# Linear attention into a squared-relu MLP: batch 2's first matmul in seven products, and one written-out order of all operations

## The chip, the cores and the metric

The kernel runs on one core of one Trainium2 chip. The metric is device time in microseconds (us) of one execution. Five engines matter: TensorE (PE in the profile, with PEld for its weight loads), VectorE (DVE), ScalarE (ACT), GpSimd (POOL) and SyncE (SP), which issues most DMAs. Each runs its own instructions strictly in the order in which the program gives them, so the order is part of the kernel.

## What is computed

Per batch (8) and head (8), with sequence 576 and head size 64, and then one MLP over all 4608 rows:

```python
q_p = concat(relu(q) * cos_w, relu(q) * sin_w)      # 576 x 128, k_p alike
kv  = k_p.T @ v                                     # 128 x 64
z   = sum(k_p)                                      # 128
x   = (q_p @ kv) / (q_p @ z + 1e-6)                 # 576 x 64 per head, 8 heads side by side: 512
h   = x @ w_in                                      # 512 -> 2048
out = (relu(h) ** 2) @ w_out                        # 2048 -> 512
```

## The kernel before

**Tiles and stages.** A batch's 576 rows are four tiles of 128 rows and a tail of 64. The four tiles of batch m make MLP step m (512 columns of x); the tails of all eight batches make a ninth step, m = 8. For a batch the kernel loads q, k and v, makes the cosine and sine features (line 339 on ScalarE, line 343 on VectorE), casts v, forms kv (line 385), transposes the query features, multiplies (line 505, the function `att_num`; for tails two batches in one call, with tiles named qpt and qptT), divides (lines 517 to 520) and transposes x. From batch 2 on the transposes are DMAs on the SP queue (line 469 for queries, line 537 for x). Loads of inputs and stores of outputs share that queue.

**First matmul.** Steps 0 to 2 use 16 units: 4 matmuls of 512 columns (line 594), a relu on ScalarE (line 603), and a square on VectorE after every four units (line 611). From step `FIRST_7` on, which is 3 (line 1405), the first matmul is done in seven products of half-size blocks instead of eight (Strassen's way, in Winograd's form): `plan_gemm1_7` runs four groups u of seven products, each 4 matmuls of 256 columns (line 671). It needs sums of weight blocks, made once (line 629), and of input blocks (line 653, four per step). In each group ScalarE copies the fifth product aside (line 1095), copies one bank into another as a seed twice (line 1078) and makes two relus (line 687); VectorE adds the fifth product to two banks (line 694), takes the maximum with zero (line 711) and squares (line 611). Two groups share four banks in two lanes.

**Second matmul.** Steps 0 and 1 are plain (lines 747 and 761). From step 2 on it is in seven products as well: 14 halves of 8 matmuls of 256 columns (line 860), sums of g blocks on VectorE (line 839), and copies and adds to the output tile (lines 1160, 1170, 1183 on ScalarE, 1166 on VectorE). The last step's version, in `plan_gemm2` for m = 8, uses more banks and stores in pieces: half stores by line 794 and quarter stores by line 802, on POOL, SP and ScalarE's queue. There the products come in the order 1, 2, 6, 5, 7, 3, 4; the result of product 7 in bank Z is added to the output (line 1166) and copied twice into other banks as seeds for product 4 (line 1221).

**Order.** Every operation is an `add` call on a planner: engine or engines, a duration, what it reads and writes, a due time. `order` lets all engines work in a model: when an engine falls free it takes the ready operation that is due first. `SHIFTS` corrects the due times of single operations, by number. An operation that may run on VectorE or ScalarE (features and casts) is taken by the engine that is free first. The result is the order in which the instructions are put out. Input transfers have landing times written in by hand (`plan.given`, `plan_pool`).

```python
i = min((i for i in waiting[e] if ready[i] <= s + 0.02), key=lambda i: (due[i], i))
```

## Time and profile before

| | |
|---|---|
| median of 3 runs | 275.87 us (275.8 to 275.89) |
| the profiled execution | 275.83 us |
| its span, first to last instruction | 274.1 us |
| mean granted TensorE clock | 0.997 |
| busy: PE, DVE, ACT, POOL | 97%, 80%, 67%, 6% of the span |
| DMA | 53.37 MB, mean 195 GB/s |

The span is the time from the first to the last instruction of the profiled execution; its device time has what lies around it as well. Busy shares are of the span. In rows of groups the two numbers before the second bar are the busy time of the group in us and the mean of one in ns; behind it stands how long the engine was idle just before, and what ended that. In timelines the first two numbers are start and length in us.

### The profile page before, as it was taken

What the parts mean: (1) busy time and instruction counts of PE and PEld (TensorE: products, weight loads), DVE (VectorE), ACT (ScalarE), POOL (GpSimd) and SP (SyncE); (2) the same over time, 40 slices, a digit from 0 to 9 for tenths busy, and PEclk for the clock granted to TensorE, in tenths of its full rate; (3) what the DMA queues carried; (4) which work ended last, traced back from release to release, by engine and by line L of the source; (5) the groups of instructions that cost most, each with busy time, mean ns of one, the idle gap of its engine ahead of it and who ended that gap; (6) DMA issues with size and microseconds to landing.
All of it is one profiled execution on the core that took longest, in us unless ns stands there. A gap on an engine that the chain in (4) does not pass through costs nothing.

```text
span 274.1 us, 6518 instructions
## 1 busy us (share of the span) xinstructions
PE 266.7 (97%) x2626; PEld 207.3 (76%) x2626; DVE 219.6 (80%) x440; ACT 182.8 (67%) x330; POOL 15.3 (6%) x29
## 2 busy tenths in 40 slices
PE   8999999999999998999999999999999999999993
PEld 3687555565445477898899898998988888888882
DVE  0974877877967999999989999998999679889401
ACT  2976741796677778779978998995645665583122
POOL 1572100000000000000000000000000000000013
PEclk9999999999999999999999999999999999999998
DMA  7999999699899999999999999845113100300134
GB/s 212 331 206 285 320 252 360 192 270 291 233 286 289 177 227 256 278 306 204 294 360 181 225 339 263 142 117 169 38 41 136 39 0 2 153 2 0 80 115 115
DMA packets 87005, 53.37 MB, mean 195 GB/s; under 512 B 56928, under 2 KB 83936, under 8 KB 86976
## 3 DMA queue, kind: packets, MB, share of 16 engines
q1 hardware_dynamic: 80448, 44.38, 62.5%
q0 software_dynamic: 5392, 8.26, 13.5%
q8 instruction: 20, 0.33, 0.5%
q10 hardware_dynamic: 1136, 0.33, 0.5%
q14 instruction: 9, 0.07, 0.1%
HBM read 36.70 MB, written 9.44 MB: 168 GB/s over the span
## 4 chain that ended last, share of the span: by engine, by line
PE 89%; DMA 5%; DVE 2%; SPq 2%; issue 0%; ACT 0%; POOL 0%; POOLq 0%; DVEq 0%
PE bank L860 29%; PE bank L671 26%; PE bank L594 12%; PE bank L747 5%; PE bank L761 5%; PE abank L385 3%; PE abank L505 3%; DMA q<-in_q_dram 3%; PE bank L721 3%; DMA qptT<-qpt 3%; SPq L237 1%; PE bank L578 1%; PE bank L478 1%; DVE x L443 0%; PE bank L542 0%
## 5 line engine op out<-in xcount | busy, mean ns | idle before, releaser
L860 PEld LDWEIGHTS <-gT 128*128 128x128 bf16 x448 | 43.2, 98 | 5.5 <-issue 0.5
L611 DVE TENSOR_TENSOR gT<-gT 128x2048 bf16<-128x2048 bf16 (+1 forms) x34 | 40.2, 1188 | 5.8 <-ACT gT L603 5.6
L860 PE MATMUL bank<-w2sb,gT 128*128 128x256 bf16 x336 | 42.1, 273 | 0.0
L671 PE MATMUL bank<-xT,w1sb 128*128 128x256 bf16 x288 | 41.9, 273 | 0.0
L687 ACT ACTIVATE gT<-bank 128x512 bf16<-128x512 f32 x48 | 28.5, 599 | 18.7 <-PE bank L671 15.7
L671 PEld LDWEIGHTS <-w1sb 128*128 128x128 bf16 x384 | 36.6, 98 | 4.3
L694 DVE TENSOR_TENSOR gT<-bank,qpTp 128x512 bf16<-128x512 f32 x48 | 31.0, 684 | 7.7 <-PE bank L671 7.2
L860 PEld LDWEIGHTS <-gs 128*128 128x128 bf16 x336 | 32.7, 98 | 3.8
L594 PE MATMUL bank<-xT,w1sb 128*128 128x512 bf16 x148 | 35.1, 379 | 0.0
L603 ACT ACTIVATE gT<-bank 128x512 bf16<-128x512 f32 x40 | 23.4, 601 | 13.2 <-PE bank L594 13.2
L1078 ACT COPY bank<-bank 128x512 f32<-128x512 f32 x48 | 27.6, 582 | 6.0 <-PE bank L671 5.4
L671 PEld LDWEIGHTS <-w1t 128*128 128x128 bf16 x288 | 28.0, 98 | 3.3
L860 PE MATMUL bank<-w2t,gs 128*128 128x256 bf16 x224 | 28.2, 273 | 0.0
L671 PE MATMUL bank<-qpTp,w1t 128*128 128x256 bf16 x192 | 27.7, 273 | 0.0
L594 PEld LDWEIGHTS <-w1sb 128*128 128x128 bf16 x148 | 13.6, 98 | 13.5
L520 DVE TENSOR_TENSOR x<-abank,rden 128x512 bf16<-128x512 f32 x30 | 20.7, 691 | 1.0
L1095 ACT COPY qpTp<-bank 128x512 f32<-128x512 f32 x24 | 13.8, 593 | 8.1 <-PE bank L671 6.6
L1166 DVE TENSOR_TENSOR ysb<-bank,y 128x512 f32<-128x512 f32 x14 | 9.6, 687 | 9.5 <-PE bank L860 9.0
L794 POOL DMA_DIRECT2D out_dram<-ysb x4 | 2.4, 613 | 238.2 <-ACT ysb L1170 234.9
L339 ACT ACTIVATE kp<-k,cos_col 128x512 bf16<-128x512 f32 x19 | 13.2, 717 | 2.9 <-DMA k<-in_k_dram 2.9
L747 PE MATMUL bank<-w2sb,gT 128*128 128x512 bf16 x64 | 14.8, 379 | 0.0
L339 ACT ACTIVATE qp<-q,cos_col 128x512 bf16<-128x512 f32 x21 | 14.7, 715 | 0.1
(119 smaller groups left out, 418.9 us busy)
## 6 DMA issues: line engine op xcount, KB each, us to landing
out_dram<-ysb SPq DMA_DIRECT2D x16, 512.0 KB, 3.2
q<-in_q_dram SPq DMA_DIRECT2D x14, 512.0 KB, 7.1
v<-in_v_dram SPq DMA_DIRECT2D x14, 512.0 KB, 5.5
k<-in_k_dram SPq DMA_DIRECT2D x12, 512.0 KB, 7.4
w1sb<-in_moe_w_in_dram POOLq DMA_DIRECT2D x4, 512.0 KB, 9.3
w2sb<-in_moe_w_out_dram POOLq DMA_DIRECT2D x4, 512.0 KB, 16.5
k<-in_k_dram SPq DMA_DIRECT2D x1, 1024.0 KB, 6.0
q<-in_q_dram POOLq DMA_DIRECT2D x1, 1024.0 KB, 12.0
```

The costliest lines, as they stand in the source:

```text
L339: eng.activation(out=dst[ps, :, lo : lo + D], in_=src[ps], func=ACTF.Relu, scale=col[ps])
L520: nc.vector.tensor_tensor(out=x[:, :], in0=n4[:, :, :, 0:D].rearrange("p b (k l) d -> p b k l d", l=2), in1=rden[:, :] .rearrange("p b (k ...
L594: nc.tensor.matmul(out=out_, lhsT=w1sb[:, kb, hb * P : (hb + 1) * P], rhs=x_block(m, kb), start=(kb == 0), stop=(kb == KB - 1),)
L603: nc.scalar.activation(out=gT_of(m)[:, hb, :], in_=bank[to][:, :], func=ACTF.Relu)
L611: nc.vector.tensor_tensor(out=g, in0=g, in1=g, op=ALU.mult)
L671: nc.tensor.matmul(out=bank[to][:, s * W : (s + 1) * W], lhsT=lhs[:, kb, (2 * u + s) * P : (2 * u + s + 1) * P], rhs=rhs[:, kb, :], start= ...
L687: nc.scalar.activation(out=g_pair(m, i, j, u), in_=bank[to][:, :].rearrange("p (s c) -> p s c", s=2), func=ACTF.Relu,)
L694: nc.vector.tensor_tensor(out=g_pair(m, i, j, u), in0=bank[to][:, :].rearrange("p (s c) -> p s c", s=2), in1=in_five(u).rearrange("p (s c) ...
L747: nc.tensor.matmul(out=bank[FIRST_Y[tt]][:, :], lhsT=gT_of(0)[:, hb, tt * P : (tt + 1) * P], rhs=w2sb[:, hb, :], start=(hb == 0), stop=(hb ...
L860: nc.tensor.matmul(out=bank[to][:, s * DM2 : (s + 1) * DM2], lhsT=lhs[:, hb, s * P : (s + 1) * P], rhs=rhs[:, hb, :], start=(fresh and hb ...
L1078: add("ACT", psum, lambda: nc.scalar.copy(out=bank[b][:, :], in_=bank[a][:, :]), r=[("bank", a)], w=[("bank", b)])
L1095: add("ACT", psum, lambda u=u, Y=Y: nc.scalar.copy(out=in_five(u), in_=bank[Y][:, :]), r=[("bank", Y)], w=five)
```

## The change

Four things change. `FIRST_7` becomes 2, so that the first matmul of step 2 is in seven products too; the weight sums stand in the plan one step earlier, and the planner has 1,302 operations where it had 1,270. Squares of whole groups may run on ScalarE (`add_square`, `squared`). In the last step the two copies of line 1221 stand ahead of the add that reads the same bank, and an operation that reads a bank now depends on those that read it before. And `order`, with its due times and `SHIFTS`, goes: `ORDER` lists all operations by number, in the order in which they are put out, each with its engine (p PE, a ScalarE, v VectorE, g POOL, s SP). Some written-in landing times are smaller; with the order fixed they reach no instruction.

The diff, cut: of the list the lines that the prediction speaks of, and its end.

```diff
-SHIFTS = {
-    62: -4, 63: -2.8, 82: -5.8, 99: -12, 100: -12.4, 101: -15.2, 102: -10, 103: -8.2, 104: -3,
...
-}
+ORDER = """
+0p 11a 17v 20v 14a 15v 18v 16a 12v 13v 22a 21v 1p 31g 27a 26v 23p 38v 19a 28p 37v 36v 2p 3p 29a 39p
+40p 43v 44a 41p 24v 45p 42a 46p 25v 47p 30v 4p 32g 57p 48a 66v 5p 49p 65a 51p 58v 6p 71a 67p 50v 7p
...
+156p 314v 92g 133a 154p 139p 134a 157v 141p 155v 93g 181v 158p 315v 174a 142a 159p 178a 317v 160p
...
+264s 288a 206v 294v 209p 286v 173p 210a 291v 287v 292a 217p 215v 226p 293a 270v 214a 223p 289v 227a
...
+319p 452a 425s 368p 342v 448a 320p 310s 251v 255a 432v 321p 431a 430v 433a 454v 322p 447v 455s 449a
...
+573s 401a 464v 417a 334p 419a 607v 465s 335p 402v 403v 336p 575s 584a 501p 470s 420v 337a 517p 338v
+588a 474p 385v 610a 476p 421v 591a 611s 583v 586a 477p 387v 592a 497v 475p 478a 498v 344v 518p 606s
+479a 502p 500v 519a 596v 482p 589v 503a 595v 594a 483p 593v 328s 585v 520a 499v 471p 504a 725s 521p
...
+599p 527v 600p 724s 510p 601a 531v 509p 512v 484a 529p 612p 511v 554p 530a 613v 480p 555a 532a 538p
+347v 513p 422v 614p 553p 515v 481p 615v 514a 556a 537p 539a 346v 616s 557p 745v 540a 617p 558p 743v
...
+1245a 1166v 1260v 1259p 1174p 1177a 1268p 1262a 1227v 1178a 1269p 1261v 1264v 1179p 1270a 1266v
+1180p 1263v 1181p 1183v 1182p 1265v 1276p 1267v 1277p 1229v 1184v 1271p 1185s 1278a 1272p 1186p
+1187p 1282p 1188a 1273a 1283p 1189s 1274g 1279p 1275g 1284a 1285a 1280p 1294p 1281a 1289p 1286v
+1295a 1288g 1290p 1287g 1298p 1297g 1291v 1296g 1293s 1299a 1301a 1292s 1300s
+"""
@@ -75,6 +106,9 @@
 
         n = len(self.ops)
         deps = set()
+        for key in r:
+            if key[0] in ("bank", "T"):
+                deps.update(self.readers.get(key, ()))
         for key in r:
             if key in self.last_write:
                 deps.add(self.last_write[key])
@@ -95,62 +129,14 @@
         self.ops.append([eng, dur, fn, deps, due, lag, at, name])
...
-    def behind(self, i, a):
-
-        return 0.0 if self.ops[i][0] == self.ops[a][0] == ("PE",) else self.ops[i][5]
-
...
-    def order(self, t0):
...
     def run(self, t0):
-        for i in self.order(t0):
-            self.ops[i][2](self.by[i])
+        names = {"p": "PE", "a": "ACT", "v": "DVE", "g": "POOL", "s": "SP"}
+        order = [(int(x[:-1]), names[x[-1]]) for x in ORDER.split()]
+        place = {i: n for n, (i, _) in enumerate(order)}
+        assert len(place) == len(order) == len(self.ops)
+        for i, e in order:
+            assert e in self.ops[i][0] and all(place[d] < place[i] for d in self.ops[i][3])
+            self.ops[i][2](e)
 
 
 @with_exitstack
@@ -602,13 +588,19 @@
     def unit_relu(m, hb, to):
         nc.scalar.activation(out=gT_of(m)[:, hb, :], in_=bank[to][:, :], func=ACTF.Relu)
 
-    def square(m, u, plain, a=0, n=4):
-
+    def squared(eng, g):
+
+        if eng is nc.scalar:
+            eng.activation(out=g, in_=g, func=ACTF.Square)
+        else:
+            eng.tensor_tensor(out=g, in0=g, in1=g, op=ALU.mult)
+
+    def square(m, u, plain, a=0, n=4, eng=nc.vector):
         if plain:
             g = gT_of(m)[:, 4 * u + a : 4 * u + a + n, :]
         else:
             g = gT_of(m).rearrange("p (j h) c -> p j h c", j=2)[:, :, 2 * u : 2 * u + 2, :]
-        nc.vector.tensor_tensor(out=g, in0=g, in1=g, op=ALU.mult)
+        squared(eng, g)
 
 
 
@@ -921,6 +913,9 @@
         engs = EITHER if only is None else (only,)
         add(engs, tuple(cost(e, n, kind) for e in engs), lambda e: fn(ENG[e]), r=r, w=w)
 
+    def add_square(n, fn, w):
+        add(EITHER, (0.06 + n * 0.00053, 0.1 + n * 0.00083), lambda e: fn(ENG[e]), w=w)
+
     def plan_k(b, j, cos=None, sin=None):
         ps, gs = parts_of(b, j)
         out = lambda x: [("kp", j, x)] if j < J else [("kpt", g, x) for g in gs]
@@ -1027,7 +1022,7 @@
             k = 2 if plain and u == 3 else 4
             if n % k == k - 1:
                 a = n % 4 + 1 - k
-                add("DVE", 0.06 + 512 * k * 0.00053, lambda u=u, a=a, k=k: square(m, u, plain, a, k),
+                add_square(512 * k, lambda e, u=u, a=a, k=k: square(m, u, plain, a, k, e),
                     w=[key for x in order[n + 1 - k : n + 1] for i in range(2) for key in g_keys(m, i, x // HB2, (x % HB2,))])
             if n % 4 == 3:
                 if not plain and u % 2:
@@ -1112,7 +1107,7 @@
             if not apart:
                 add("DVE", 0.34, lambda u=u: in_max(m, u), w=g(1, 0) + g(1, 1))
             if not apart:
-                add("DVE", 1.14, lambda u=u: square(m, u, False), w=[key for i in range(2) for j in range(2) for key in g(i, j)])
+                add_square(2048, lambda e, u=u: square(m, u, False, eng=e), w=[key for i in range(2) for j in range(2) for key in g(i, j)])
             if u % 2:
                 plan_g_sums(m, 2 * u - 2, 2 * u + 2)
 
@@ -1213,13 +1208,13 @@
         prod(5, V)
         five(V)
         prod(7, Z)
-        last(Z, 1, 1, True)
-        store_half(1, 1, ("POOL", "POOL"))
 
         for sub in range(2):
             add("ACT", cost("ACT", 256, "psum"),
                 lambda sub=sub: nc.scalar.copy(out=half_bank(2 + sub)[:, sub, :], in_=half_bank(Z)[:, sub, :]),
                 r=[("bank", Z)], w=[("bank", 2 + sub)])
+        last(Z, 1, 1, True)
+        store_half(1, 1, ("POOL", "POOL"))
         prod(3, Y)
         last(Y, 0, 1, True)
         store_half(0, 1, ("SP", "SP"))
@@ -1265,7 +1260,7 @@
     T0, TM = 1.2, 15.4
 
     for key, at in (
-        (("k", 0), 6.8), (("k", 1), 6.8), (("kt", 0), 7.1), (("q01",), 8.9), (("vt", 0), 9.5),
+        (("k", 0), 6.8), (("k", 1), 6.8), (("kt", 0), 7.1), (("q01",), 8.9), (("vt", 0), 9.3),
         (("v", 0), 10.2), (("v", 1), 11.5), (("q23",), 13.0),
     ):
         plan.given[key] = at
@@ -1309,7 +1304,7 @@
         plan_q(0, j, src=[("q01",)])
         plan_qT_pe(0, j, j, 10.0 + 0.3 * j, "DVE" if j == 0 else "ACT")
     add("POOL", 0.1, gate, r=[("vt", 0)], due=0.0)
-    for i, at in enumerate((16.2, 19.4, 21.9, 24.5)):
+    for i, at in enumerate((15.6, 19.1, 21.1, 23.7)):
         plan_pool(at, lambda i=i: load_w1(i, 4), [("w1", i)])
     for half in range(2):
         for i in range(2):
@@ -1348,14 +1343,14 @@
         plan_num(0, j, TM + 0.5 + 0.8 * (j - 2))
         plan_x_pe(0, j, 2 + j, TM + 1.8 + 0.8 * (j - 2), None)
 
-    plan_pool(27.1, lambda: load_main("q", 1, nc.gpsimd), [("q", 0), ("q", 1), ("q01",), ("q23",)])
-    plan_pool(29.9, lambda: load_w2(0, 4), [("w2", 0)])
-    plan_pool(32.9, lambda: load_main("k", 1, nc.gpsimd), [("k", 0), ("k", 1)])
-    plan_pool(33.3, lambda: load_tail("k", 1, nc.gpsimd), [("kt", 1)])
-    plan_pool(35.6, lambda: load_w2(1, 4), [("w2", 1)])
-    plan_pool(38.6, lambda: load_main("v", 1, nc.gpsimd), [("v", 0), ("v", 1)])
-    plan_pool(39.0, lambda: load_tail("v", 1, nc.gpsimd), [("vt", 1)])
-    for i, at in ((2, 41.3), (3, 43.9)):
+    plan_pool(27.0, lambda: load_main("q", 1, nc.gpsimd), [("q", 0), ("q", 1), ("q01",), ("q23",)])
+    plan_pool(29.5, lambda: load_w2(0, 4), [("w2", 0)])
+    plan_pool(32.3, lambda: load_main("k", 1, nc.gpsimd), [("k", 0), ("k", 1)])
+    plan_pool(32.7, lambda: load_tail("k", 1, nc.gpsimd), [("kt", 1)])
+    plan_pool(35.1, lambda: load_w2(1, 4), [("w2", 1)])
+    plan_pool(38.1, lambda: load_main("v", 1, nc.gpsimd), [("v", 0), ("v", 1)])
+    plan_pool(38.6, lambda: load_tail("v", 1, nc.gpsimd), [("vt", 1)])
+    for i, at in ((2, 41.0), (3, 43.7)):
         plan_pool(at, lambda i=i: load_w2(i, 4), [("w2", i)])
     for s in FIRST_S:
         plan_first(s)
@@ -1363,7 +1358,7 @@
         n = hb - 4 * len(FIRST_S) // 2
         plan_unit(0, hb, n % 4, TM + len(FIRST_S) * dt0 + n * dt0 / 2)
         if n % 4 == 3:
-            add("DVE", 0.06 + 2048 * 0.00053, lambda u=hb // 4: square(0, u, True),
+            add_square(2048, lambda e, u=hb // 4: square(0, u, True, eng=e),
                 w=[key for x in range(hb - 3, hb + 1) for i in range(2) for key in g_keys(0, i, x // HB2, (x % HB2,))])
     for j in range(J):
         plan_q(1, j)
@@ -1402,7 +1397,7 @@
     t = tB + 4.0
     dC = 0.98
     win[0] = (t, t + 14.0)
-    FIRST_7, STRIDE, SHIFT = 3, 2.0, -6.0
+    FIRST_7, STRIDE, SHIFT = 2, 2.0, -6.0
     if FIRST_7 == 1:
         plan_w1_sums(28.0)
         plan_gemm1_7(1, t, 0.5)
```

101 lines of the change are left out of this document (54 added, 47 removed), and 37 rows, old and new, of the table SHIFTS.

## Prediction

> **What bounds the kernel now.** I read the page's engine totals first, then the chain that ended last, then what TensorE waited for, and last the stages.
>
> ```profile
> span 274.1 us, 6518 instructions
> ...
> PE 266.7 (97%) x2626; PEld 207.3 (76%) x2626; DVE 219.6 (80%) x440; ACT 182.8 (67%) x330; POOL 15.3 (6%) x29
> ...
> PE 89%; DMA 5%; DVE 2%; SPq 2%; issue 0%; ACT 0%; POOL 0%; POOLq 0%; DVEq 0%
> ```
>
> TensorE (PE) is the bound: 89% of the chain is its own work. So time is saved only by fewer product columns, or by closing the few holes in its stream. Two pieces of the chain give the pitch at which matmuls follow each other, without the pipeline's tail that each record's mean carries:
>
> ```profile
> 33.70 6.04 PE bank L747 x28
> 247.73 6.99 PE bank L860 x64
> ```
>
> A 512-column matmul costs 6.04/28 = 0.2157 us, a 256-column one 6.99/64 = 0.1092 us. The two engines beside it, by stage (columns: stretch, then busy us of PE, PEld, DVE, ACT, POOL, clock, DMA):
>
> ```profile
> 60.00:80.00 20.00, 20.00 (x133) 9.49 (x130) 17.38 (x36) 12.75 (x22) 0.00 (x0) 1.00 1.05 278
> 80.00:100.00 20.00, 20.00 (x164) 11.08 (x163) 15.99 (x32) 15.34 (x28) 0.00 (x0) 1.00 1.03 241
> 100.00:130.00 30.00, 29.27 (x331) 25.94 (x329) 28.84 (x59) 23.66 (x43) 0.00 (x0) 1.00 1.16 253
> 130.00:200.00 70.00, 70.00 (x805) 62.74 (x804) 65.40 (x133) 60.03 (x110) 0.00 (x0) 1.00 0.83 209
> ```
>
> VectorE (DVE) is nearly as full as TensorE from 100 us on. It is what could become the bound. Between 60 and 100 us it has 2.62 + 4.01 = 6.6 us free. These are the holes of TensorE's stream that I found:
>
> ```profile
> PE abank L505 <- DMA qptT<-qpt: 0.7, 1, 0.7
> PE bank L547 <- ACT xT L552: 0.5, 1, 0.5
> PE bank L860 <- ACT bank L1221: 0.4, 1, 0.4
> ...
> 103.41 1.04 PE L860 MATMUL bank<-w2t,gs 128*128 128x256 bf16 x8
> 105.18 0.44 PE L505 MATMUL abank<-kvz,qptT 128*64 128x65 bf16 x16 [0.73 <-DMA qptT<-qpt]
> ...
> 51.08 1.76 PE L578 MATMUL bank<-xT,w1sb 128*128 128x256 bf16 x12
> ```
>
> The waits are understated by the drain of the last matmul, so I take starts and pitches: 103.41 + 8 × 0.1092 = 104.28 to 105.18 is a hole of 0.90 us (the tail rows' product of batches 2 and 3 waits for its transposed queries). At 51 us twelve matmuls take 1.76 where 12 × 0.1092 plus a drain of 1.04 − 8 × 0.1092 = 0.17 makes 1.48: a hole of 0.28.
>
> **Part 1: seven products for batch 2.** Batch 2's first matmul was 16 units of 4 matmuls at 512 columns: 64 × 0.2157 = 13.80 us. As seven products it is 4 groups × 7 × 4 = 112 at 256 columns: 112 × 0.1092 = 12.23 us. TensorE saves **1.57 us**. The price lies on the other two engines:
>
> ```profile
> L687 ACT ACTIVATE gT<-bank 128x512 bf16<-128x512 f32 x48 | 28.5, 599 | 18.7 <-PE bank L671 15.7
> ...
> L694 DVE TENSOR_TENSOR gT<-bank,qpTp 128x512 bf16<-128x512 f32 x48 | 31.0, 684 | 7.7 <-PE bank L671 7.2
> ...
> L1078 ACT COPY bank<-bank 128x512 f32<-128x512 f32 x48 | 27.6, 582 | 6.0 <-PE bank L671 5.4
> ...
> L1095 ACT COPY qpTp<-bank 128x512 f32<-128x512 f32 x24 | 13.8, 593 | 8.1 <-PE bank L671 6.6
> ...
> L611 DVE TENSOR_TENSOR gT<-gT 128x2048 bf16<-128x2048 bf16 x32 | 38.9, 1220 | 5.8 <-ACT gT L603 5.6
> ...
> L711 DVE TENSOR_SCALAR gT<-gT 128x1024 bf16<-128x1024 bf16 x24 | 9.6, 420 | 0.0
> ...
> L653 DVE TENSOR_TENSOR qpTp<-xT 128x512 bf16<-128x512 bf16 x6 | 2.5, 420 | 0.0
> ```
>
> VectorE gets 8 adds × 0.684 + 4 maxima × 0.420 + 4 input sums × 0.420 = 8.8 us. ScalarE (ACT) loses 8 of 16 relus and gets 8 seed copies and 4 copies of the fifth product: 8 × (0.582 − 0.599) + 4 × 0.593 = +2.2 us. The four weight sums existed already; they only move earlier. What hides the 8.8 us is the free VectorE time of 60 to 100 us, and part 2. Where that cover is gone, each microsecond too many is a microsecond of TensorE, since relus, adds and squares free the banks that the next product needs.
>
> **Part 2: squares that may run on ScalarE.** No square runs there in this trace. I bound one of 2,048 elements from the nearest rows:
>
> ```profile
> L603 ACT ACTIVATE gT<-bank 128x512 bf16<-128x512 f32 x40 | 23.4, 601 | 13.2 <-PE bank L594 13.2
> ...
> L805 ACT COPY ysb<-bank 128x256 f32<-128x256 f32 x2 | 0.7, 373 | 1.3 <-PE bank L860 1.3
> ```
>
> The slope is (601 − 373)/256 = 0.89 ns an element, so 0.601 + 1,536 × 0.00089 = 1.97 us; four separate 512s, 2.40, is the upper end, and VectorE's own 1.22 the lower. I take 1.97, by the slope. In the new list 11 of 34 squares carry an "a": VectorE gives back 11 × 1.22 = 13.4 us and ScalarE takes 21.7. Three of the 11 stand in batch 3's group and one in batch 2's, which is 4.9 us off VectorE in the crowded stretch, so 8.8 − 4.9 = 3.9 us must fit into the 6.6 free; I cost it at nothing. Their cover on ScalarE, by the example of entry 532a: between it and ScalarE's next entry, 514a, stand three groups of 4 matmuls and one of 8, 20 × 0.1092 = 2.18 us, longer than the square. In 100 to 130 us ScalarE has 30 − 23.66 = 6.3 us idle. Where that cover is gone, a seed copy comes up to 1.97 us late and the product that adds to it with it.
>
> The Trainium skill, "ScalarE: Activation LUTs", section "Rules for kernel authors", speaks against this: multiplies belong on VectorE, per element up to about three times faster in bf16. By these rows the ratio is 1.97/1.22 = 1.6. By the rule as a sum the 11 moves waste 11 × 0.75 = 8.3 us of engine time; by the stages above they are spent on the engine that has idle time and taken from the one that has none.
>
> **Part 3: the fixed order.** I read the list entry by entry (numbers count the add calls). It keeps each engine's work and the SP queue's order much as they were; three places differ in what I can price. The new planned load times (27.1 to 27.0 and the like) and the new dependency between readers of one bank reach no instruction once the order is written down: nothing.
>
> (a) The 0.90 hole. The new list issues the same transpose (470s) and wants its result in 471p. Between them stand 517, 474, 476, 477, 475, 518, 502, 482, 483: three groups of 4 and six halves of 8 matmuls, 3 × 4 × 0.1092 + 6 × 8 × 0.1092 = 6.55 us. The queue before it is as before: transposes and v loads.
>
> ```profile
> 98.12 7.01 DMA qptT<-qpt
> ...
> DMA to landing us min/median/max: 3.7/5.6/7.0
> ```
>
> With 7.01 again, 0.46 us of hole stays and **0.44** is saved. Ends: with 5.6 all 0.90 go; with a queue a little fuller nothing does.
>
> (b) The end. Before, the copies of line 1221 stood behind the add of line 1166, since both read one bank in the order of the code:
>
> ```profile
> 266.34 1.04 PE L860 MATMUL bank<-w2sb,gs 128*128 128x256 bf16 x8
> 266.60 1.51 DVE L1166 TENSOR_TENSOR ysb<-bank,y 128x512 f32<-128x512 f32 x2 [7.77 <-PE bank L860]
> 267.32 0.63 ACT L1221 COPY bank<-bank 128x256 f32<-128x256 f32 x2 [1.94 <-DVE ysb L1166]
> 267.73 1.91 PE L860 MATMUL bank<-w2t,gT 128*128 128x256 bf16 x16 [0.35 <-ACT bank L1221]
> 268.13 1.34 SPq L794 DMA_DIRECT2D out_dram<-ysb  x2
> 269.67 0.37 ACT L805 COPY ysb<-bank 128x256 f32<-128x256 f32 x1 [0.50 <-PE bank L860]
> 270.07 0.50 SPq L802 DMA_DIRECT2D out_dram<-ysb  x1
> 270.08 0.55 ACTq L802 DMA_DIRECT2D out_dram<-ysb  x1
> ...
> out_dram<-ysb SPq DMA_DIRECT2D x1, 64.0 KB, 2.5
> out_dram<-ysb ACTq DMA_DIRECT2D x1, 64.0 KB, 2.7
> ```
>
> The hole is 266.34 + 8 × 0.1092 = 267.21 to 267.73: **0.52** saved, since the copies now go first. But the new list puts product 4's first half (1294p) ahead of product 3 (1289p, 1290p), so product 3 ends only one half, 8 × 0.1092 = 0.87 us, before TensorE's end E. Its add then ends at E − 0.87 + 0.04 + 0.69 = E − 0.14, SP issues two stores for 1.34 us, and the last quarter store, which is behind them on SP, starts at E + 1.22 and lands at E + 3.72. Before, E was 267.73 + 1.91 = 269.64 and the last store landed at 270.08 + 2.7 = E + 3.14. So the end gives back **0.58**.
>
> (c) The hole at 51 us: the four copies that free the output banks are spread so that other products (226p) stand between; I take 0.28 saved, nothing if they come as late as before.
>
> The start: the new list puts the second batch of divisions and a transpose of tile 3 ahead of the first product, which moves work without removing it; the last query tile's transfer ends the wait either way.
>
> ```profile
> 12.97 0.88 DVE qp L343 x2
> ...
> 16.59 0.61 PE L721 MATMUL bank<-xT,w1sb 128*128 128x128 bf16 x8
> ```
>
> Between the landing and the first product lie 3.6 us of dependent steps; I take no change, and 0.5 either way, the size of the one wait named there (line 547 on line 552's copy).
>
> (d) New waits. An order tuned in a model is right only as far as the model's durations are. The order of before, made in the same model, left 0.90 + 0.52 + 0.28 = 1.7 us of holes after the start. Nothing excludes the same again in new places; nothing demands it. Between 0 (what closes is in (a) to (c) already) and 1.7 I take 0.4, between the smallest and the middle hole. What is late next where a hole closes is TensorE's own next product: no other engine's row stands closer.
>
> **Sum**, against the profiled execution's 275.83 us (the median is 275.87, so no correction; 1.73 us lie around the span): 275.83 − 1.57 − 0.44 − 0.52 + 0.58 − 0.28 + 0.4 = **274.0 us**.
>
> **The rivals.**
> - *Everything closes:* the transposes land in 5.6 us, no new wait, the start gains 0.5: 274.0 − 0.46 − 0.4 − 0.5 = 272.6. For it: the holes of before were few, so the model that ordered them knows the durations well. Against it: the same queue. 0.17.
> - *The order gives the saving back:* new holes of 1.7 instead of 0.4 and the 0.90 hole stays: 274.0 + 1.3 + 0.44 = 275.7, no change that can be told. 0.12.
> - *Slower: VectorE becomes the bound* where batch 2's seven products meet batch 3's sums. Price: if none of the 3.9 us finds the free time of 60 to 100, 274.0 + 3.9 = 277.9. It decides from the point where VectorE's idle there falls to nothing while PE shows holes before line 671. Against it: 6.6 us are free and the list starts the first products of batch 2 (368p) inside the second matmul of batch 1. 0.08.
> - *Slower: table loads.* If each square reloaded ScalarE's table and the next relu loaded it back, 22 loads:
>
> ```profile
> L283 ACT ACT_TABLE_LOAD x1 | 1.3, 1283 | 2.2 <-DVE bias_pi L281 2.2
> ```
>
> Batch 3's three squares would then cost 3 × (1.97 + 2.57) = 13.6 us of ScalarE against 6.3 idle: about 7 us late, 281. The one load here serves sine, relu and copy. 0.02. The Trainium skill, "ScalarE: Activation LUTs", section "Table sets: the hidden batching unit", names relu, copy, identity and abs as in every set, square not; no run here shows it.
>
> **How the numbers follow.** Forecast 274.0 (own range 273.2 to 275.2): 0.61. With the rivals at 0.17, 0.12, 0.08 and 0.02. The range takes in the first rival's 272.6 and the second's 275.7 and leaves out the slower ones: 272.5 to 275.9. A measurement tells about 0.2%, 0.55 us, from no change. Faster (forecast and first rival) 0.78, same 0.12, slower 0.10.
>
> **What would show it.** Line 594 has 64 matmuls fewer and line 671 112 more, with TensorE still gapless from 60 to 100 us: part 1 right. A hole before line 505's qptT product near 102 us of under 0.5: (a) right. The last SP store issued over a microsecond after TensorE's end: (b) right. Wrong would be: a hole before line 671 released by VectorE or a ScalarE square, more than one table load, or a first product later than 17.5 us.

## The result and the profile after

The changed kernel takes 273.95 us (median of 8 runs, 272.37 to 274.6); the kernel before took 275.84 beside it (275.21 to 276.28). The ratio is 0.9928, 95% interval 0.9903 to 0.9952: faster by 0.7%, at the predicted 274.0. The profiled execution is one of the quicker ones, so its ledger is larger than the median's.

| us | before | after |
|---|---|---|
| profiled execution | 275.83 | 272.8 |
| span | 274.1 | 271.0 |
| first product of the first matmul | 16.59 | 17.25 |
| TensorE's end, E | 269.64 | 266.44 |
| last store landed, behind E | 3.14 | 3.38 |

The page of the changed kernel, the lines that answer to those of before:

```profile
span 271.0 us, 6628 instructions
...
PE 265.0 (98%) x2674; PEld 212.0 (78%) x2674; DVE 221.0 (82%) x458; ACT 197.3 (73%) x332; POOL 15.9 (6%) x29
...
PE 91%; DMA 3%; SPq 2%; DVE 1%; POOL 1%; issue 0%; ACT 0%; POOLq 0%
```

TensorE still bounds it, with 98% in place of 97%. ScalarE has 14.5 us more, VectorE only 1.4. The groups of instructions say why (the changed kernel's line numbers are 5 to 15 lower: 580 was 594, 589 was 603, 596 was 611, 663 was 671, 679 was 687, 686 was 694; line 594 is now the square on ScalarE):

```profile
L679 ACT ACTIVATE gT<-bank 128x512 bf16<-128x512 f32 x56 | 32.5, 598 | 17.4 <-PE bank L663 17.0 <-DVE kp L329 0.3
...
L596 DVE TENSOR_TENSOR gT<-gT 128x2048 bf16<-128x2048 bf16 (+1 forms) x23 | 26.9, 1172 | 0.8 <-ACT gT L589 0.3
L594 ACT ACTIVATE gT<-gT 128x2048 bf16<-128x2048 bf16 x11 | 21.0, 1912 | 0.1
...
L580 PE MATMUL bank<-xT,w1sb 128*128 128x512 bf16 x84 | 19.9, 379 | 0.0
```

Line 580 has 84 matmuls where line 594 had 148, and 11 squares have gone over to ScalarE at 1.912 us each. The list makes a third move, the other way: of the cosine and sine features ScalarE has 73 and VectorE 73 (lines 325 and 329), where they had 80 and 66, and of the main value casts 11 and 17 (line 347), where they had 15 and 13. So VectorE, which gave up the 11 squares, got work in return. All that TensorE waited for, by the view of waits (the first row, at the very start, stood before too):

```profile
PE abank L353 <- DVE zeros L248: 1.2, 1, 1.2
PE bank L464 <- DVE qpTp L481: 0.3, 1, 0.3
```

The three waits of before on queries, on line 547's copy and on line 1221 are gone. The timeline where the tail rows' product of batches 2 and 3 stands:

```profile
96.69 1.93 SPq L455 DMA_TRANSPOSE qptT<-qpt  x1
```

```profile
101.53 1.91 PE L852 MATMUL bank<-w2sb,gT 128*128 128x256 bf16 x16
103.37 0.45 PE L491 MATMUL abank<-kvz,qptT 128*64 128x65 bf16 x16
```

101.53 + 16 × 0.1092 = 103.28, and the product starts at 103.37: the hole of 0.90 is closed, and the transposes landed 4.0 us after their issue and not 7.0:

```profile
qptT<-qpt SPq DMA_TRANSPOSE x1, 4.0
```

In all eleven profiles with the new list (the experiments' included) these transposes land 3.6 to 4.7 us after their issue; in the kernel before and in b_tail, an experiment below that keeps its order, 7.0 and 6.75. Why they land sooner is not shown: what SP issues just ahead of them, a transpose of x and a load of value tails, is the same in both.

And the end:

```profile
263.65 1.91 PE L852 MATMUL bank<-w2sb,gs 128*128 128x256 bf16 x16
...
265.40 1.04 PE L852 MATMUL bank<-w2t,gT 128*128 128x256 bf16 x8
265.60 0.69 DVE L1161 TENSOR_TENSOR ysb<-bank,y 128x512 f32<-128x512 f32 x1 [1.31 <-PE bank L852]
...
266.32 1.34 SPq L786 DMA_DIRECT2D out_dram<-ysb  x2
...
267.76 0.60 SPq L794 DMA_DIRECT2D out_dram<-ysb  x1
```

263.65 + 16 × 0.1092 = 265.40: no hole. The last SP store is issued at 267.76, 1.32 behind E, and lands 2.06 later.

In the prediction's way of reckoning, starts and pitches, TensorE's stream has 0.42 us of hole left at 15.9 (0.89 before, in two), 0.13 at 28.2 and 0.18 at 39.2, and none over 0.15 behind that. For the start all time beyond the pitches counts, from the first matmul at 1.19 to 24 us: 4.10 us before and 3.82 after. The holes at 15.9 and 19.6 have shrunk by 0.62, and what stands ahead of 15 us, among the fill-in matmuls on zeros (38 in both kernels), has grown by 0.34. The first product comes 0.66 later all the same, since other work stands ahead of it. The ledger of the profiled executions, in us:

| step | predicted | shown |
|---|---|---|
| part 1, seven products | −1.57 | −1.57 (by counts and pitches) |
| (a) hole at the query product | −0.44 | −0.90 |
| (b) hole of line 1221 | −0.52 | −0.52 |
| (b) the end gives back | +0.58 | +0.24 |
| (c) hole at 51 | −0.28 | −0.28 |
| the start | 0 | −0.28 |
| (d) new waits | +0.4 | +0.31 |
| sum | −1.83 | −3.00, measured −3.03 |

So the forecast's number is that of the median, but its sum isn't that of the profile, which is 1.2 us better. Something takes those 1.2 us back in most executions. That is what the later experiments look for.

### The profile page after: what moved, and what is told of

The parts are those of the page before. It is cut to its first block, busy times and chain, and to the rows that moved or that the text cites. A ratio compares the mean times of both kernels' runs of the same rounds, so it can differ in the third digit from the quotient of the medians.

```text
span 271.0 us, 6628 instructions
## 1 busy us (share of the span) xinstructions
PE 265.0 (98%) x2674; PEld 212.0 (78%) x2674; DVE 221.0 (82%) x458; ACT 197.3 (73%) x332; POOL 15.9 (6%) x29
## 4 chain that ended last, share of the span: by engine, by line
PE 91%; DMA 3%; SPq 2%; DVE 1%; POOL 1%; issue 0%; ACT 0%; POOLq 0%
PE bank L663 32%; PE bank L852 30%; PE bank L580 7%; PE bank L739 5%; PE bank L753 5%; PE abank L371 3%; PE abank L491 3%; DMA q<-in_q_dram 3%; PE bank L713 3%; SPq L223 1%; PE bank L564 1%; PE bank L464 1%; PE bank L528 0%; DVE x L429 0%; POOL out_dram L786 0%
## 5 line engine op out<-in xcount | busy, mean ns | idle before, releaser
L663 PE MATMUL bank<-xT,w1sb 128*128 128x256 bf16 x336 | 48.2, 273 | 0.0
L663 PEld LDWEIGHTS <-w1sb 128*128 128x128 bf16 x448 | 42.8, 98 | 6.6
L679 ACT ACTIVATE gT<-bank 128x512 bf16<-128x512 f32 x56 | 32.5, 598 | 17.4 <-PE bank L663 17.0
L686 DVE TENSOR_TENSOR gT<-bank,qpTp 128x512 bf16<-128x512 f32 x56 | 36.6, 684 | 6.9 <-PE bank L663 4.8
L596 DVE TENSOR_TENSOR gT<-gT 128x2048 bf16<-128x2048 bf16 (+1 forms) x23 | 26.9, 1172 | 0.8 <-ACT gT L589 0.3
L594 ACT ACTIVATE gT<-gT 128x2048 bf16<-128x2048 bf16 x11 | 21.0, 1912 | 0.1
L580 PE MATMUL bank<-xT,w1sb 128*128 128x512 bf16 x84 | 19.9, 379 | 0.0
L663 PE MATMUL bank<-xT,w1t 128*128 128x256 bf16 x112 | 16.6, 273 | 0.0
L663 PE MATMUL bank<-zeros,w1sb 128*128 128x256 bf16 x112 | 16.2, 273 | 0.0
L753 PE MATMUL bank<-w2sb,gT 128*128 128x512 bf16 x64 | 15.4, 379 | 0.0
L739 PE MATMUL bank<-w2sb,gT 128*128 128x512 bf16 x64 | 15.3, 379 | 0.0
```

Of the source, the lines that this page charges most:

```text
L580: nc.tensor.matmul(out=out_, lhsT=w1sb[:, kb, hb * P : (hb + 1) * P], rhs=x_block(m, kb), start=(kb == 0), stop=(kb == KB - 1),)
L594: eng.activation(out=g, in_=g, func=ACTF.Square)
L596: eng.tensor_tensor(out=g, in0=g, in1=g, op=ALU.mult)
L663: nc.tensor.matmul(out=bank[to][:, s * W : (s + 1) * W], lhsT=lhs[:, kb, (2 * u + s) * P : (2 * u + s + 1) * P], rhs=rhs[:, kb, :], start= ...
L679: nc.scalar.activation(out=g_pair(m, i, j, u), in_=bank[to][:, :].rearrange("p (s c) -> p s c", s=2), func=ACTF.Relu,)
L686: nc.vector.tensor_tensor(out=g_pair(m, i, j, u), in0=bank[to][:, :].rearrange("p (s c) -> p s c", s=2), in1=in_five(u).rearrange("p (s c) ...
```

## The experiments

### Is the seven-product part worth its 1.57 us?

First the changed kernel again, as it is, as a yardstick.

> The changed kernel again, for a second profile, because its runs lie between 272.37 and 274.6 us and the first profile shows one of the fast ones (272.8, TensorE almost without a hole after 40 us). Theory: the order leaves waits on DMA landings about as much room as the landings scatter, so an execution of 273.5 us or more shows holes of 0.3 to 1.2 us in TensorE's stream that are absent at 272.8, ended by a DMA. Rival: the scatter is in the start (input landing) or in the end (stores), and TensorE's stream between the first product and the last is equally long in both, within 0.2 us.

Measured: 273.99 us (6 runs), ratio 0.9923 [0.9901, 0.9946]; profiled 273.63. Its trace is that of the first one from 41 us on. Ahead of that it has a hole of 0.66 us at 19.4, in front of a product that waits for the first weight, which the first one lacks, and one of 0.53 at 39.7 in front of batch 1's key-value products, where the first has 0.18. TensorE ends at 267.27 and not at 266.44, and these 0.83 us are the whole difference of the two executions, as the theory had it:

```profile
PE bank L713 <- DMA w1sb<-in_moe_w_in_dram: 0.5, 1, 0.5
PE abank L371 <- DVE vext L347: 0.4, 1, 0.4
```

Then the new list with batch 2 in 16 units again (the groups' entries replaced by the units', all else in its place):

```diff
-    FIRST_7, STRIDE, SHIFT = 2, 2.0, -6.0
+    FIRST_7, STRIDE, SHIFT = 3, 2.0, -6.0
```

> The new order and all else of the change, but batch 2's first matmul in 16 units again, put in the places of the products. Theory: TensorE is the bound and the seven products are worth their 1.57 us in full: 1.4 to 1.8 us slower than the changed kernel (about 275.5 against 273.95). Rival: VectorE and ScalarE had become the bound there, and without the 8.8 us of VectorE work that the products bring the kernel is as fast as the changed one, within 0.4 us.

Measured: 275.88 us (12 runs), ratio 0.9998 [0.9984, 1.0013]; profiled 274.98. That is 1.89 above the changed kernel by the medians, 1.35 by the two profiles, with a new hole of 0.67 at 203.9 that the one has and the other not. The part is worth about what the pitches say, and the list without it is worth nothing that can be told in the median.

### Where would the gain be without the squares on ScalarE, and without the list?

All 11 squares back on VectorE, in the same places:

```diff
-555a 532a 538p
+555a 532v 538p
...
```

> The changed kernel with all 11 ScalarE squares back on VectorE, at the same places in the order. Theory: VectorE has hardly any idle time where eight of them stand (100 to 180 us), 11 x (1.22) = 13.4 us come back to it, and TensorE then waits for it: 2 to 5 us slower than the changed kernel. Rival: the moved squares were not needed, the idle time elsewhere takes them: within 0.4 us.

Measured: 279.61 us (6 runs), ratio 1.012 [1.0102, 1.0137], 5.6 above the changed kernel; more than the 2 to 5 expected. TensorE now waits for VectorE all along:

```profile
PE bank L739 <- DVE qpTp L472: 0.8, 2, 0.5
PE bank L852 <- DVE ysb L763: 0.6, 1, 0.6
PE bank L663 <- DVE qpTp L645: 0.6, 1, 0.6
...
PE abank L491 <- DVE x L506: 0.5, 1, 0.5
```

VectorE's busy time rose by only 232.4 − 221.0 = 11.4 us, of 277.7. It isn't full on the average; it is late in the places where a bank or an operand hangs on it.

The kernel before with seven products for batch 2 and nothing else (the planner's priorities stay, its shifts renumbered to the same operations):

> The kernel before with batch 2's first matmul in seven products, and nothing else of the change: squares on VectorE, the planner's priorities and its shifts kept for the same operations. TensorE has 1.57 us less work, VectorE 8.8 us more. Theory, the saving can be had only with room on VectorE and an order made for it: waits on VectorE's operands take more than it gives, 1 to 5 us slower than the kernel before, 277 to 281 us. Rival, seven products by themselves carry the gain and the order only what is left over: 274.3 to 275 us.

Measured: 280.72 us (5 runs), ratio 1.0208 [1.0184, 1.0231]. TensorE's work is shorter, and the kernel 5 us longer:

```profile
PE abank L373 <- DVE x L508: 2.4, 1, 2.4
PE bank L659 <- DVE qpTp L641: 1.6, 1, 1.6
```

The 2.4 are one case in full. TensorE's numerator ends at 180.6 and VectorE, in its fixed order, runs two maxima and a square before the division that frees the bank; the key-value products start at 183.0:

```profile
180.22 0.41 PE L493 MATMUL abank<-kvz,qpT 128*128 128x65 bf16 x8
183.00 1.13 PE L373 MATMUL abank<-vext,kp 128*128 128x65 bf16 x32 [2.38 <-DVE x L508]
```

```profile
180.03 0.75 DVE L699 TENSOR_SCALAR gT<-gT 128x1024 bf16<-128x1024 bf16 x2
180.69 1.22 DVE L599 TENSOR_TENSOR gT<-gT 128x2048 bf16<-128x2048 bf16 x1
181.83 0.16 DVE L505 TENSOR_SCALAR den<-abank 128x8 f32<-128x8 f32 x1
182.02 0.20 DVE L506 RECIPROCAL rden<-den 128x8 f32<-128x8 f32 x1
182.26 0.69 DVE L508 TENSOR_TENSOR x<-abank,rden 128x512 bf16<-128x512 f32 x1
```

The shifts had been set for other work, so this isn't the best that a planner could do with seven products. But the five kernels make a table: seven products with the old planner 280.7, with the list 279.6, with the list and 11 squares on ScalarE 274.0; sixteen units, 275.8 before and 275.9 with list and squares. With this list, the squares are what lets the saving out; an order made for seven products with every square on VectorE was not run.

### What does the end give back?

The changed kernel with product 3 ahead of both halves of product 4, as before the change:

```diff
-1280p 1294p 1281a 1289p 1286v 1295a 1288g 1290p
+1280p 1281a 1289p 1286v 1288g 1290p 1294p
-1298p 1297g
+1298p 1295a 1297g
```

> The changed kernel with the last step's product 3 ahead of both halves of product 4 again, so that SP's two half stores go out 0.87 us earlier ahead of the last quarter store. Theory: the last store starts 0.8 to 0.9 us earlier after TensorE's end and the kernel is 0.5 to 0.7 us faster. Rival: something behind the last landing sets the end and nothing changes, within 0.2 us.

Measured: 273.14 us (5 runs), ratio 0.9895 [0.9878, 0.9911] beside 0.9923 [0.9901, 0.9946]; the intervals meet. The traces show no gain: E to the end of the span is 4.56 us, 4.58 in the changed kernel's second profile, as the last store, issued earlier, takes 2.7 us to land in place of 2.05. A later kernel with the same tail, e_kv_gateq_tail, has 4.41, so the traces leave room for at most 0.2. The median speaks for one side and the traces for the other, and this stays open.

The other way round, the kernel before, in its planner's own order written out, with only the two copies of line 1221 ahead of the add:

```diff
-        last(Z, 1, 1, True)
-        store_half(1, 1, ("POOL", "POOL"))
         for sub in range(2):
             add("ACT", cost("ACT", 256, "psum"),
...
+        last(Z, 1, 1, True)
+        store_half(1, 1, ("POOL", "POOL"))
```

> The kernel before, in its planner's own order written out, with one thing changed: the two ScalarE copies of the last product's seed (line 1221 of before) stand ahead of the last VectorE add that reads the same bank, as in the changed kernel. Batch 2 in sixteen products, squares on VectorE. Theory of the prediction's terms (b): the hole of 0.52 us ahead of the last product goes, and the end gives back 0 to 0.6: between 275.3 and 275.9 us, with the last landing 3.1 to 3.7 us behind TensorE's end. By the rows of the changed kernel (3.38 there, 3.14 before), 275.5. Rival, the hole moves on to the next wait of the tail: 275.8, with a hole of 0.3 to 0.5 left in the last 10 us.

Measured: 276.23 us (12 runs), ratio 1.0023 [1.0006, 1.0039]: slower if anything, and both expectations missed. The hole is gone, but the add comes behind the copies and its stores with it. The end of this kernel:

```profile
266.67 1.04 PE L851 MATMUL bank<-w2sb,gs 128*128 128x256 bf16 x8
266.93 0.63 ACT L1213 COPY bank<-bank 128x256 f32<-128x256 f32 x2 [1.22 <-PE bank L851]
...
267.55 1.91 PE L851 MATMUL bank<-w2t,gT 128*128 128x256 bf16 x16
267.60 1.29 DVE L1160 TENSOR_TENSOR ysb<-bank,y 128x512 f32<-128x512 f32 x2 [8.44 <-ACT bank L1213]
268.58 1.20 POOL L785 DMA_DIRECT2D out_dram<-ysb  x2 [3.96 <-DVE ysb L1160]
...
268.91 1.34 SPq L785 DMA_DIRECT2D out_dram<-ysb  x2
...
269.77 1.07 POOL L793 DMA_DIRECT2D out_dram<-ysb  x2
269.90 0.55 ACTq L793 DMA_DIRECT2D out_dram<-ysb  x1
270.35 0.56 SPq L793 DMA_DIRECT2D out_dram<-ysb  x1
```

266.67 + 8 × 0.1092 = 267.54: no hole. But eight stores are begun between 268.58 and 270.35, within 1.8 us, and the last two take 3.5 and 3.3 us to land, 4.23 behind E in place of 3.14. In the kernel before the eight lay within 2.5 us, in the changed one within 3.2 (264.58 to 267.76), and there the last takes 2.06. So the copies ahead of the add don't give the gain of (b) by themselves. What the list adds is not the place of product 4: e_tail has product 3 ahead of it again and keeps 4.56. In e_tail and in the changed kernel the first of the last two adds begins 2.84 us ahead of E (264.40 and 263.60), in b_tail 1.86 ahead (267.60), and the stores follow the adds. Whether that would do without the copies' new place was not run.

### What takes 1.2 us back in most executions?

A third profile of the changed kernel, with a theory: GpSimd issues the first weight's loads behind a 64x1 copy that waits for batch 0's value tail, and VectorE holds that copy up.

> The changed kernel as it is, on the same chip as the next three. What is to be tested with it: GpSimd's 64x1 copy of line 218, behind which the four loads of the first weight stand in GpSimd's queue, took 0.18 us before the change (begun at 9.13), 0.20 in the run with batch 2 in sixteen products (8.80), 0.57 in the first profile of the changed kernel (9.94), 1.53 in its second (9.57), 1.67 (9.58) and 1.95 (9.42) in two others with the changed order; VectorE runs one SBUF-to-SBUF instruction behind the other in that time. Theory, the copy is held up by VectorE's unbroken row: where it begins behind 9.3 us it takes 0.5 to 2 us, the first weight's quarters land 0.5 to 1.3 us later than in the kernel before (15.46, 18.99, 20.96, 23.52), and the median of the runs is 273.5 to 274.3 us. Rival, the landings scatter by themselves: the copy's length and the landings go apart.

Measured: 274.19 us (6 runs), ratio 0.9942 [0.9926, 0.9959]; profiled 274.22. The copy took 0.23 us here and the loads were late all the same, so the theory as put fell. What GpSimd did, in the kernel before, in this profile and in the changed kernel's second (start, us):

```profile
9.13 0.18 POOL L232 COPY got<-vt 64x1 f32<-64x1 f32 x1 [7.26 <-DMA vt<-in_v_dram]
9.25 3.38 POOL L292 DMA_DIRECT2D w1sb<-in_moe_w_in_dram  x4
```

```profile
8.85 0.23 POOL L218 COPY got<-vt 64x1 f32<-64x1 f32 x1 [6.98 <-DMA vt<-in_v_dram]
9.02 4.99 POOL L278 DMA_DIRECT2D w1sb<-in_moe_w_in_dram  x4
```

```profile
9.57 1.53 POOL L218 COPY got<-vt 64x1 f32<-64x1 f32 x1 [7.70 <-DMA vt<-in_v_dram]
11.04 3.15 POOL L278 DMA_DIRECT2D w1sb<-in_moe_w_in_dram  x4
```

In the second of these the hold-up has moved from the copy to the first issue (2.50 us by the records, 1.04 before). And it is a late load that costs: batch 1's values landed at 40.20, and TensorE stood 1.24 us in front of the products that need them:

```profile
38.72 1.24 PE L739 MATMUL bank<-w2sb,gT 128*128 128x512 bf16 x5
41.04 1.13 PE L371 MATMUL abank<-vext,kp 128*128 128x65 bf16 x32 [1.08 <-DVE vext L347]
```

The copy made by VectorE in place of GpSimd, behind its second query cosine (it writes an element that the load overwrites):

```diff
-        nc.gpsimd.tensor_copy(out=got[rows(0), :], in_=kqv["vt", 0][rows(0), 0, 0:1])
+        nc.vector.tensor_copy(out=w1sb[rows(0), 0, 0:1], in_=kqv["vt", 0][rows(0), 0, 0:1])
```

> The changed kernel, and the copy on which the first weight's loads wait is made by VectorE, behind its second query cosine of batch 0 (it writes one element of the weight's tile, which the load then overwrites; nothing is left out). VectorE has one 64x1 copy more, about 0.1 us. Theory of the held-up copy: the copy is done by 10.2 us at the latest and the first load is issued there, 0.3 to 1.1 us earlier than in the four profiles with 10.45 to 11.31; the quarters land by as much earlier, so that the hole of 0.66 us at 19.44 and that of 0.53 at 39.72 of the second profile go: 0.6 to 1.2 us below the changed kernel's median of the same call, so about 272.8 to 273.4, and a narrower scatter. Rival, the landings scatter by themselves: within 0.3 us of the changed kernel.

Measured: 274.0 us (6 runs), ratio 0.9941 [0.9927, 0.9955], no gain. The copy is short, but VectorE reaches it at 10.07, and the four issues run from 10.52 to 13.85: late by another road.

The copy back on GpSimd and reading batch 0's first query load, which lands earlier and more evenly:

```diff
-        nc.gpsimd.tensor_copy(out=got[rows(0), :], in_=kqv["vt", 0][rows(0), 0, 0:1])
+        nc.gpsimd.tensor_copy(out=got[rows(0), :], in_=kqv["q", 0][rows(0), 0, 0, 0:1])
```

> The changed kernel, with GpSimd's small copy, behind which the first weight's loads stand, reading batch 0's first query load (landed at 8.75 to 9.16 in nine profiles) in place of the value tail (8.67 to 9.89). What the last four runs left of the theory: GpSimd is held up by VectorE's unbroken row between 9.3 and 11.1 us, in the copy (1.53 us) or in the issue behind it (2.50 us where the copy took 0.23), and what counts is when the second weight load is issued: 10.04, 10.28 and 10.53 gave landings of 18.46, 18.99 and 19.18; 11.44 to 12.21 gave 19.43 to 20.29. Theory: the copy begins at 8.9 to 9.2 in every execution and the second load is issued at 10.0 to 10.6 in most; the median is 0.4 to 1.0 us below the changed kernel's, ratio 0.989 to 0.992. Rival: GpSimd is held up at its first issue all the same (as at 9.02 in one profile), the second load is issued at 11 or later, and the ratio stays at 0.992 to 0.994.

Measured: 273.64 us (6 runs), ratio 0.993 [0.9908, 0.9951]. The copy began at 8.88 and took 1.24 us; the second load was issued at 11.40. The rival's case: the data that it waits for is not the cause.

The wait itself put off, with a part of the second matmul in front of it:

```diff
-164p 96g
+164p 165p 96g
...
-191p 165p 192a
+191p 192a
...
-340v 193p 261s 166p 194v
+340v 261s 166p 193p 194v
```

> The changed kernel with two TensorE operations at other places: the eighth of batch 0's sixteen parts of the second matmul (0.86 us of products whose operands are there) goes ahead of batch 1's three key-value products, which wait for batch 1's value load, and the first numerator of batch 1 goes behind the ninth. Theory of the late loads: the hole in front of those products follows the landing of the load (0.18 us with 38.78, 0.53 with 39.62, 0.65 with 39.36, 1.24 with 40.20), and the part put ahead fills up to 0.86 of it: that hole is 0 to 0.4 us, and the median lies 0.3 to 0.8 us below the changed kernel's, at a ratio to the kernel before of 0.990 to 0.992 against 0.9928, 0.9923 and 0.9942. Rival, the wait only moves on to the parts behind, which need the next load of the second weight (41 to 43 us): within 0.2 us of the changed kernel.

Measured: 274.07 us (10 runs), ratio 0.9943 [0.9922, 0.9965]. The hole in front of the key-value products is gone, with the load at 39.48, and another of 0.59 us stands at 44.3, in front of the next numerator (the numerators now follow each other more closely than VectorE's divisions), and the first weight's load, at 17.86, cost 0.78 at 17.1:

```profile
PE bank L713 <- DMA w1sb<-in_moe_w_in_dram: 0.6, 1, 0.6
...
PE abank L491 <- DVE x L506: 0.4, 1, 0.4
```

The rival had the right outcome, but for another wait than the one it named. All three edits (this, the query load and the tail) in one kernel:

> The two edits of the two runs before together with that of the tail (product 3 ahead of both halves of product 4, as in the kernel before). If late loads are what parts the changed kernel's slower executions from its best (272.37 us), the median comes near that: 272.3 to 273.0, ratio 0.987 to 0.990, with TensorE free of holes over 0.3 us behind 20 us. Rival, each edit opens a hole elsewhere: 273.5 to 274.5.

Measured: 273.77 us (6 runs), ratio 0.9928 [0.9907, 0.9948], again the rival: GpSimd's copy took 2.09 us from 8.97, and the wait that e_kv's rival named is here as well, beside the new one:

```profile
PE abank L491 <- DVE x L506: 0.4, 1, 0.4
PE bank L739 <- DMA w2sb<-in_moe_w_out_dram: 0.4, 1, 0.4
```

Last, the suspected cause undone: VectorE's and ScalarE's work up to 13 us dealt out and ordered as before the change, all other places of the list kept:

```diff
-0p 11a 17v 20v 14a 15v 18v 16a 12v 13v 22a 21v 1p 31g 27a 26v 23p 38v 19a 28p 37v 36v 2p 3p 29a 39p
-40p 43v 44a 41p 24v 45p 42a 46p 25v 47p 30v 4p 32g 57p 48a 66v 5p 49p 65a 51p 58v 6p 71a 67p 50v 7p
...
+0p 1p 11a 12v 13v 14a 15v 16v 17a 18v 19a 20v 21v 22a 31g 38v 26a 27v 23p 36v 37a 28p 24v 25a 29v
+30a 43v 44a 2p 3p 39p 40p 41p 45p 42a 46p 47p 4p 32g 57p 48a 66v 5p 49p 65a 51p 58v 6p 71a 67p 50v
...
```

From 9 us on VectorE then runs a query cosine, the tail cast, a query sine, a value cast and two copies out of TensorE's banks, where the list had two query cosines and three casts in one row.

> The changed kernel, with VectorE's and ScalarE's work up to 13 us (batch 0's key features, first two query features, value casts and first four transposed-query copies) dealt out and ordered as in the kernel before; every other place of the list is kept, TensorE's among them. What the last runs left: GpSimd's copy and its first issue behind it took 1.22 to 1.87 us together in two profiles of the old order (1.03 behind 9.25 and 1.44 behind 9.09 for the issue alone), 1.24 to 2.93 in ten of the new one, whether the copy waited for the value tail or for the query load, and the second weight load was issued at 10.28 and 10.53 with the old, 11.40 to 12.26 in nine of ten with the new. Theory, it is how VectorE's SBUF-to-SBUF work lies between 9 and 11 us: with the old row the second load is issued at 10.0 to 10.6, the quarters land at 15.4 to 15.9, 18.4 to 19.2, 20.9 to 21.2 and 23.5 to 23.7 and batch 1's value load before 38.9, the holes at 19.4 and 39.5 are under 0.2 us, and the ratio to the kernel before is 0.988 to 0.991 (272.5 to 273.3 us). Rival, the hold-up comes from elsewhere and falls where it falls: second load at 11 or later, ratio 0.992 to 0.994.

Measured: 273.03 us (6 runs, 272.93 to 274.18), ratio 0.9907 [0.9889, 0.9925]: in the range that the theory gave, four of the six within 0.1 us of each other. The value tail landed late in the profiled one (9.46), and GpSimd got through nevertheless:

```profile
9.51 0.67 POOL L219 COPY got<-vt 64x1 f32<-64x1 f32 x1 [7.64 <-DMA vt<-in_v_dram]
10.13 3.31 POOL L279 DMA_DIRECT2D w1sb<-in_moe_w_in_dram  x4
```

The second load was issued at 11.18, not at the 10.0 to 10.6 expected; its landing (19.14) is inside the expected stretch and the hole at 19.4 is gone. But batch 1's values landed at 39.29 and not before 38.9, and the hole at 39.6 is 0.30 and not under 0.2; the second issue behind 11 us is what the rival expected, the median is not. Nine profiles side by side (us; the first two columns from the rows above and their like, the landings from the DMA records):

| kernel | VectorE's first row | copy begun | fourth issue done | second quarter landed | batch 1's values landed | hole in front of them |
|---|---|---|---|---|---|---|
| before | old | 9.13 | 12.63 | 18.99 | 37.98 | 0 |
| b_tail | old | 8.72 | 13.01 | 19.18 | 37.97 | 0 |
| e_start | old | 9.51 | 13.44 | 19.14 | 39.29 | 0.30 |
| e_units | new | 8.80 | 12.60 | 18.46 | 37.61 | 0 |
| after | new | 9.94 | 13.99 | 19.43 | 38.78 | 0.18 |
| e_gateq | new | 8.88 | 13.85 | 19.57 | 39.37 | 0.62 |
| a1 | new | 9.57 | 14.19 | 20.08 | 39.62 | 0.53 |
| e_tail | new | 9.58 | 14.35 | 20.16 | 39.50 | 0.33 |
| a2 | new | 8.85 | 14.01 | 19.94 | 40.20 | 1.24 |

From the beginning of the copy to the end of the fourth issue it is 3.5, 4.3 and 3.9 us with the old row, and 3.8, 4.1, 5.0, 4.6, 4.8 and 5.2 with the new one. Of the five profiles that the table leaves out, four have the new row (fourth issue done at 13.85 to 14.57, second quarter landed at 19.67 to 20.37, values at 39.36 to 39.70), and b_seven the old one (13.25 and 19.29, but values only at 39.53).

Is it VectorE that holds GpSimd up? Its row in the changed kernel's second profile, whose copy began at 9.57 and took 1.53 us:

```profile
10.31 0.75 DVE L382 CAST vext<-v 128x512 bf16<-128x512 f32 x2
11.47 0.69 DVE L382 CAST vext<-v 128x512 bf16<-128x512 f32 x1 [0.42 <-DMA v<-in_v_dram]
```

The row ends at 10.31 + 0.75 = 11.06, and the copy at 9.57 + 1.53 = 11.10. So it is everywhere: in each of the 13 profiles with this copy it ends 0.04 to 0.06 us behind the end of a VectorE instruction, and in the five in which it took over 1.3 us (all with the new row) that is the last one of the unbroken row. In e_units, where GpSimd got through, VectorE's instructions are the longer ones: two pairs took 1.00 and 0.93 us that take 0.87 and 0.75 in the changed kernel's first two profiles. So the copy waits for VectorE, as plainly as times can show it.

The rest of the chain is looser. Second quarters that land late go with late issues, but batch 1's values landed late in e_start and b_seven as well, whose issues were early. And that the new row is what takes back 1.2 us in most executions is likely and not settled: e_start's median is in the theory's range, but its interval overlaps those of the changed kernel, e_units got through the new row, and e_tail, with the new row and its loads as late as any, has a median of 273.14, as low as e_start's. What would settle it, more profiles of the two rows, wasn't made.

The Trainium skill, "SBUF — State Buffer", section "Who interferes with whom", has a mechanism for it: VectorE's copies, casts and tensor-scalars between SBUF and SBUF can take, for a whole instruction, a port pair that GpSimd needs, and GpSimd then stands still. The Trainium skill's section "SBUF: two separate sides" on that page adds that this also keeps GpSimd from writing the descriptors of its own DMAs. The rows fit both: 0.18 to 2.09 us for a 64x1 copy, 1.04 and 2.50 for the same issue; for the issue nothing but the one long case speaks. That one of the two waits for several instructions of the other, and not for one, is in the rows and not in the Trainium skill.

## Why the prediction came out

**What bounds it:** right. TensorE's share rose to 98%, and but for the end's 0.24 every step of the ledger is a change in its product columns or its holes.

**Part 1:** right, 1.57 by the counts, 1.35 to 1.89 by the kernel without it. Its two prices were right as well (56 − 48 = 8 more adds at 0.684, 8 more seed copies). The price of nothing for the cover held: in the first profile the view of waits has TensorE nowhere waiting for VectorE behind 17 us, and VectorE's busy time of 60 to 100 us rose by 3.9 us, from 33.4 to 37.3, as much as had to fit there. But the cover was put in the wrong order of weight: the prediction named VectorE's idle time of 60 to 100 us first and the squares second. With the idle time alone, in either order, the kernel is slower by 3.8 to 5.0 us than before. The rival "VectorE becomes the bound" at 277.9 was priced for the case with the squares moved; without them it is 279.6 and 280.7.

**Part 2:** right in mechanism and close in size. The square takes 1.912 us, 1.97 was taken by the slope; against VectorE's 1.22 that is 1.6 times. There is one table load in the whole trace, so the rival with a load per square is out. The Trainium skill's rule on multiplies ("ScalarE: Activation LUTs", "Rules for kernel authors") would have cost the gain here: moving the 11 squares by it is e_squares_dve.

**Part 3, each engine's work:** the sentence that the list keeps it much as it was is wrong. By the prices of parts 1 and 2 ScalarE gets 2.2 + 21.7 = 23.9 us and VectorE 8.8 − 13.4 = −4.6; shown are +14.5 and +1.4, mostly by the features and casts that went from ScalarE to VectorE. It cost TensorE nothing that the first profile shows.

**(a):** mis-sized. The term that was mis-sized is the 7.01 us taken for the transposes' landing; they took 4.0, so 0.90 and not 0.44 was saved. The lower end, "with 5.6 all 0.90 go", was what happened. Why they landed sooner stays open.

**(b):** the hole's 0.52 is right. The last SP store was issued 1.32 behind E, 1.22 was predicted. The mis-sized term is its landing: 2.06 us, not the 2.5 carried over from an end where eight stores were begun within 2.5 us. So 0.24 was given back, not 0.58. In the old order, b_tail shows, the same edit gives back more than it saves.

**(c):** right, as far as the missing wait tells. **The start:** 0.28 better in the profile, inside the ±0.5.

**(d):** 0.31 in the first profile against 0.4, but 1.2 in the second (0.66 + 0.53) and 1.75 in the third (0.51 + 1.24), which lie nearer the median. The step that failed is the reading of "new waits": the prediction took their size from the holes of the old order and looked for their cause in the model's durations. The new ones of over 0.3 us sit in the first 41 us, and hang on loads that land late though the list moves no load in any queue. Why they do is shown in part: GpSimd, which issues them, is held up by VectorE's row.

So the number is in part luck. The error in (d), 0.8 and 1.35 in the second and third profile, goes against those in (a), (b) and the start, 0.46 + 0.34 + 0.28 = 1.08 together. At the median, e_units says, the list without the seven products is worth nothing that can be told, where the prediction's terms behind part 1 add up to −0.26: what the median shows is part 1.

## What to carry to other kernels

When one engine is full, a product that it saves is paid for on its neighbours: reckon for each instruction of theirs what TensorE waits for behind it, not the neighbour's idle share. VectorE with 80% busy was the bound as soon as 8.8 us were put on it without taking others away.

An order of instructions on one engine can delay another engine that shares no data with it, as VectorE's row did with GpSimd's copy. Look at the first loads' issue and landing in several executions before a gain is put down to a median.

A store's landing time went with the crowd around it, and a transpose's changed by 3 us with the order. Take such a time from a row with the same company, or keep both ends.

## What the runs showed of the hardware that was not expected

- The 64x1 copy on GpSimd took 0.18 to 2.09 us, and in 13 of 13 profiles ended 0.04 to 0.06 us behind the end of a VectorE instruction; the same issue of a load behind it took 0.90 to 2.50.
- The last 64 KB store on SP took 2.06, 2.5 and 3.3 us to land where the last eight stores were begun within 3.2, 2.5 and 1.8 us; the same transposed queries took 4.0 and 7.0.
- A ScalarE square of 128x2048 bf16 in place takes 1.912 us, and needs no table load next to relu, copy and sine.
